# Three products for one: the order of the high and low halves in a chain of retention and two feed-forward layers

## The chip, the cores and the metric

The kernel runs on one core of a Trainium2 chip. The metric is the device time of one execution in microseconds (us); the median of several runs counts. A profile is one further execution, recorded by the hardware profiler.

## The reference

Three stages follow one another. Retention takes q, k and v (4 batches, 8 heads, 576 positions, 64 features per head), weights the scores with powers of a decay per head and multiplies by v. Its output, 2304 tokens by 512 features, goes through a gated layer of 1536 hidden features and a second layer of 2048 hidden features.

```python
# _attn_ref
scores = scale * np.matmul(q, k.transpose(0, 1, 3, 2))
ret = scores * Dmat[None, :, :, :]
return np.matmul(ret, v).astype(np.float32)
# _moe_ref
xn = x / rms * rms_g
g = xn @ w_gate
silu = g * (1.0 / (1.0 + np.exp(-g)))
val = xn @ w_val
return (silu * val @ w_out).astype(np.float32)
# _moe2_ref
h = x @ w_in
g = np.where(pos, h, np.where(neg, 0.0, (h + beta) ** 2 / (4.0 * beta)))
return (g @ w_out).astype(np.float32)
```

## The kernel before

Most products use a number form that is read at one column per cycle but has few bits (`F32R`). To keep the precision, each operand is split into a high half, which is the operand rounded to that form, and a low half, the rest. The helper `split` (lines 294 to 296) has ScalarE write the high half and VectorE subtract it from the source for the low one, so a low half is always finished behind its high half. A product of two operands is then three products into one accumulator: high by high, and twice high by low. The helper `three` (lines 544 to 547) issues them. Its arguments are the stationary operand's halves `wh` and `wl` and the moving operand's halves `xh` and `xl`. It is called in four places:

- `front` (line 557): the gate and the value product of the first layer. Weights stand, the activations `x_t` move (tile `xall`), four triples for the gate and four for the value in each step.
- `back_a` (line 569): the first layer's second product. Weights stand, the hidden activations move (tile `h`). The products are those of the step before.
- `product` (lines 674 to 677): the second layer's first product, seven block products of a Strassen-like scheme, two triples each. Weights stand (`wf`, in the tile `wt`), sums of the activations move (`xall`).
- `back_b` (line 688): the second layer's second product. Here the activations stand (`hh` and `hl`, tile `h`) and the weights move (`wprep`).

The first layer runs over five blocks of 512, 512, 384, 512 and 384 tokens, and in each over 12 steps of 128 hidden features: 24 products in `front`, 12 in `back_a`. Within these steps the pieces of retention for later blocks are put in, and weights for the second layer are prepared. The second layer runs over three batches of 768 tokens with 8 steps each (`step_b`, lines 714 to 764): 42 products of 384 columns in `product`, 36 of 512 in `back_b`. At a change of block `split_x` writes the next block's halves; at a change of batch `split_xb` does.

No order of an engine's queue is written out directly. All calls go to a `Plan`, which knows an estimated cost of each operation and its dependencies. `issue` (lines 139 to 200) plays them through and lets each engine take an operation that is ready: TensorE the first in program order, the others the one with the earliest due time. A due time is computed backwards from the operations that need the result, with TensorE's in their program order (lines 152 to 160). Products into one accumulator stay in order. An operation is taken as ready if it is so within 100 ns (`HOLD`). The order found is then issued to the chip, where each engine works its queue in order and waits on semaphores.

Pairs of products with one stationary operand exist before too: `rms_rstd` (lines 509 and 510) multiplies the high and the low half of the sums of squares by `ones_r`, one behind the other.

```python
nc.tensor.matmul(ps[:, :T], lhsT=ones_r, rhs=hi, start=True, stop=False)
nc.tensor.matmul(ps[:, :T], lhsT=ones_r, rhs=lo, start=False, stop=True)
```

Of the kernel before, what the change touches and what calls it, by code (L numbers as in the profile page):

```python
# [211 lines left out]
def moe_chain_kernel(ctx: ExitStack, tc: tile.TileContext, att, tail, wa, wb, dmat, gq, gk, out):  # L212
    nc = Plan(tc.nc)
# [329 lines left out]

    def three(ps, wh, wl, xh, xl, first, last, **k):
        nc.tensor.matmul(ps, lhsT=wh, rhs=xh, start=first, stop=False, **k)
        nc.tensor.matmul(ps, lhsT=wl, rhs=xh, start=False, stop=False, **k)
        nc.tensor.matmul(ps, lhsT=wh, rhs=xl, start=False, stop=last, **k)

    def front(s, j):
        t = steps[s][1]  # L550
        T = BLOCKS[t]
        fh, fl = a_weights(s, j)
        hi, lo = x_t[t]
        ps = fr_p.tile([P, 512], F32, tag="fr", name="fr")
        for k in range(KD):
            q = slice(k * P, (k + 1) * P)
            three(ps[:, :T], fh[:, q], fl[:, q], hi[:, k, :T], lo[:, k, :T], k == 0, k == KD - 1)
        return ps

    def back_a(s, i):  # L560
        _, t, f = steps[s]
        T = BLOCKS[t]
        oh, ol = a_weights(s, 2)
        hh, hl = h_t[s]
        if f == 0 and i == 0:
            acc_t[t] = [ps_p.tile([P, 512], F32, tag=f"acc{i}") for i in range(KD)]
        ps = acc_t[t][i]
        q = slice(i * P, (i + 1) * P)
        three(ps[:, :T], oh[:, q], ol[:, q], hh[:, :T], hl[:, :T], f == 0, f == NA - 1)
        if f == NA - 1:  # L570
            o = next(o_next)
            nc.scalar.copy(out=o[:, :T], in_=ps[:, :T])
            nc.scalar.dma_start(out=x2d[:, i, STARTS[t]:STARTS[t] + T], in_=o[:, :T])
# [97 lines left out]
    def product(q, j, ps, first, last):  # L671
        w = wf_t[q].rearrange("p (j w k n) -> p j w k n", w=2, k=2, n=P)
        for k in range(2):
            three(
                ps, w[:, j, 0, k], w[:, j, 1, k], xs[:, j, 0, k], xs[:, j, 1, k], first and k == 0, last and k == 1,
                skip_group_check=True,
            )
# [213 lines left out]
```

## Time and profile before

| | |
|---|---|
| time, median of 3 runs | 920.0 us (919.15 to 921.18) |
| the profiled execution's span | 920.9 us |
| products (MATMUL) and their loads (LDWEIGHTS) | 5098 and 5098 |
| TensorE products in flight | 904.3 us, 98% |
| TensorE loads | 797.7 us, 87% |
| VectorE | 576.2 us, 63% |
| ScalarE | 482.3 us, 52% |
| GpSimd | 70.3 us, 8% |

In the profile PE is TensorE with its products, PEld its loads of the stationary operand, which lie beside products, DVE is VectorE, ACT ScalarE, POOL GpSimd, SP the queue that issues most transfers. Products overlap in the records, so the time that one takes in a stream is read from the distance of starts and not from its duration. In the names, `fr<-xall,wt` is a first product of either layer, `acc<-h,wt` a second product of the first layer, `acc<-wprep,h` and `at<-wprep,h` a second product of the second layer, `at<-h,ones_r` the pair with the ones. All operations have one line (L135), that of the planner's call; so one goes by tiles.

### The profile page before, as it was taken

How to read it: one execution, taken by the hardware profiler on the slowest of the kernel's cores; microseconds unless marked ns; L12 is line 12 of the kernel's file. 1: busy time of each engine (PE TensorE's matmuls, PEld its weight loads, DVE VectorE, ACT ScalarE, POOL GpSimd, SP SyncE). 2: the span in 40 equal slices, each digit the busy share in tenths (PEclk: the TensorE clock that was granted, in tenths of full speed). 3: DMA queues.
4: the chain of work that ended last, by engine and by line, in shares of the span. 5: the costliest groups of instructions: out<-in, count | busy, mean ns of one | idle time of the engine just before them, and what ended most of it. 6: DMA issues, size and time to landing. Idle time of an engine off the chain costs nothing.

```text
span 920.9 us, 13342 instructions
## 1 busy us (share of the span) xinstructions
PE 904.3 (98%) x5098; PEld 797.7 (87%) x5098; DVE 576.2 (63%) x929; ACT 482.3 (52%) x858; POOL 70.3 (8%) x80
## 2 busy tenths in 40 slices
PE   8799999999999999999999999999999999999998
PEld 7578888888889998888899998989888998989896
DVE  3978888888988888855658645434734345434343
ACT  3446665555765576533545454445654455644443
POOL 4620001310014001100000000000000000000000
PEclk9999999999999999999999999999999999999999
DMA  9679976988769984642254386646765454755432
GB/s 364 229 261 314 308 278 235 331 331 325 283 240 378 387 291 150 234 150 94 103 202 153 104 329 243 216 160 216 251 222 194 169 191 170 266 165 213 159 137 69
DMA packets 51647, 209.94 MB, mean 228 GB/s; under 512 B 5632, under 2 KB 11392, under 8 KB 47488
## 3 DMA queue, kind: packets, MB, share of 16 engines
q1 hardware_dynamic: 45392, 199.51, 61.2%
q10 hardware_dynamic: 6192, 9.59, 2.8%
q8 instruction: 40, 0.66, 0.3%
q14 instruction: 23, 0.19, 0.1%
HBM read 167.14 MB, written 41.94 MB: 227 GB/s over the span
## 4 chain that ended last, share of the span: by engine, by line
PE 92%; DVE 4%; DMA 2%; ACT 2%; issue 1%; ACTq 0%
PE fr L135 50%; PE acc L135 31%; PE at L135 11%; DMA out_dram<-o 1%; DMA att<-in_att_dram 1%; DVE xraw L135 1%; DVE xall L135 0%; DVE t L135 0%; DMA gk_sb<-in_gk_dram 0%; DVE w L135 0%; DVE wt L135 0%; ACT att L135 0%; DVE state L135 0%; DVE wsum L135 0%; DVE wpair L135 0%
## 5 line engine op out<-in xcount | busy, mean ns | idle before, releaser
L135 PE MATMUL fr<-xall,wt 128*128 128x384 f32 (+1 forms) x2424 | 512.1, 356 | 3.6 <-DVE xall L135 1.3
L135 PEld LDWEIGHTS fr<-xall,wt 128*128 128x128 f32 x2424 | 436.8, 188 | 53.5 <-DVE xall L135 2.4
L135 PE MATMUL acc<-h,wt 128*128 128x512 f32 (+1 forms) x708 | 158.1, 370 | 0.1
L135 PE MATMUL acc<-wprep,h 128*128 128x512 f32 x576 | 155.7, 394 | 0.5 <-ACT h L135 0.5
L135 PEld LDWEIGHTS acc<-h,wt 128*128 128x128 f32 x708 | 128.4, 188 | 18.2 <-ACT o L135 0.6
L135 DVE TENSOR_TENSOR wt<-w,wt 128x512 fp32r<-128x512 f32 (+1 forms) x118 | 114.4, 985 | 17.7 <-ACT wt L135 17.3
L135 PEld LDWEIGHTS acc<-wprep,h 128*128 128x128 f32 x576 | 106.6, 188 | 15.8 <-ACT h L135 0.9
L135 ACT CAST wt<-w 128x512 fp32r<-128x512 f32 (+1 forms) x118 | 96.7, 835 | 42.1 <-PE acc L135 23.6
L135 DVE TENSOR_TENSOR t<-fr,t 128x512 f32<-128x512 f32 (+1 forms) x120 | 76.3, 636 | 58.0 <-PE fr L135 29.5
L135 ACT ACTIVATE att<-att 128x384 f32<-128x384 f32 x156 | 79.2, 523 | 30.1 <-DVE att L135 18.2
L135 ACT CAST h<-t 128x512 fp32r<-128x512 f32 (+1 forms) x60 | 34.6, 577 | 79.3 <-DVE t L135 79.3
L135 DVE TENSOR_TENSOR att<-fr,att 128x384 f32<-128x384 f32 x48 | 26.6, 555 | 70.6 <-ACT att L135 69.6
L135 PE MATMUL at<-wprep,h 128*128 128x512 f32 x288 | 70.3, 392 | 0.0
L135 DVE TENSOR_TENSOR h<-att,h 128x384 fp32r<-128x384 f32 x96 | 52.8, 554 | 23.7 <-ACT h L135 23.1
L135 ACT ACTIVATE t<-fr 128x512 f32<-128x512 f32 (+1 forms) x60 | 33.3, 554 | 59.0 <-PE fr L135 58.7
L135 PEld LDWEIGHTS at<-wprep,h 128*128 128x128 f32 x288 | 53.7, 188 | 10.4
L135 ACT COPY att<-fr 128x384 f32<-128x384 f32 x48 | 23.0, 479 | 75.7 <-PE fr L135 70.2
L135 ACT CAST h<-att 128x384 fp32r<-128x384 f32 x96 | 48.7, 512 | 21.2 <-DVE att L135 20.0
L135 DVE SCALAR_TENSOR_TENSOR att<-att,att 128x384 f32<-128x384 f32 x48 | 26.8, 558 | 42.3 <-ACT att L135 42.3
L135 DVE TENSOR_TENSOR h<-t,h 128x512 fp32r<-128x512 f32 (+1 forms) x60 | 38.0, 634 | 14.2 <-ACT h L135 13.9
L135 DVE SCALAR_TENSOR_TENSOR att<-att,fr 128x384 f32<-128x384 f32 x24 | 13.3, 553 | 36.8 <-ACT att L135 36.8
L135 DVE TENSOR_TENSOR xall<-xraw,xall 128x512 fp32r<-128x512 f32 (+2 forms) x32 | 25.9, 828 | 2.8 <-ACT xall L135 2.4
(144 smaller groups left out, 672.5 us busy)
## 6 DMA issues: line engine op xcount, KB each, us to landing
w<-wa SPq DMA_DIRECT2D x48, 768.0 KB, 4.5
wprep<-wod SPq DMA_DIRECT2D x48, 512.0 KB, 4.0
wt<-wfd SPq DMA_DIRECT2D x24, 1024.0 KB, 5.2
wt<-wfd SPq DMA_DIRECT2D x24, 768.0 KB, 4.5
stage<-in_wb_dram SPq DMA_DIRECT2D x32, 512.0 KB, 6.4
wfd<-wprep SPq DMA_DIRECT2D x8, 1792.0 KB, 7.0
att<-in_att_dram SPq DMA_DIRECT2D x26, 512.0 KB, 5.8
stage<-in_wa_dram SPq DMA_DIRECT2D x26, 512.0 KB, 5.5
```

The lines of the kernel that those rows point to most:

```text
L135: call = lambda: getattr(real, method)(*args, **kwargs)
```

## The change

In `three` the second and the third product change places. Before, the stationary operand's low half by the moving operand's high half came second; now the stationary operand's high half by the moving operand's low half does. The flag that closes the accumulation moves along. Nothing else is edited; the planner computes its order anew.

```diff
     def three(ps, wh, wl, xh, xl, first, last, **k):
         nc.tensor.matmul(ps, lhsT=wh, rhs=xh, start=first, stop=False, **k)
-        nc.tensor.matmul(ps, lhsT=wl, rhs=xh, start=False, stop=False, **k)
-        nc.tensor.matmul(ps, lhsT=wh, rhs=xl, start=False, stop=last, **k)
+        nc.tensor.matmul(ps, lhsT=wh, rhs=xl, start=False, stop=False, **k)
+        nc.tensor.matmul(ps, lhsT=wl, rhs=xh, start=False, stop=last, **k)
```

## Rows read from the trace of the kernel before

**Rows 1.** The page: busy us by engine, and the granted clock in 40 slices.

```profile
PE 904.3 (98%) x5098; PEld 797.7 (87%) x5098; DVE 576.2 (63%) x929; ACT 482.3 (52%) x858; POOL 70.3 (8%) x80
PEclk9999999999999999999999999999999999999999
```

**Rows 2.** Timeline of TensorE, steady first-layer steps: start, length, operation, count.

```profile
100.52 5.60 PE L135 MATMUL fr<-xall,wt 128*128 128x512 f32 x24
108.68 5.60 PE L135 MATMUL fr<-xall,wt 128*128 128x512 f32 x24
...
313.41 4.32 PE L135 MATMUL acc<-h,wt 128*128 128x384 f32 x24
317.57 2.75 PE L135 MATMUL fr<-xall,wt 128*128 128x384 f32 x13
```

**Rows 3.** TensorE's waits, longest first; last row: the only one from 80 to 545.

```profile
PE at L135 <- DMA att<-in_att_dram: 2.2, 1, 2.2
...
PE fr L135 <- DVE wt L135: 0.5, 1, 0.5
```

**Rows 4.** Timeline of TensorE, one step of the second layer, cut to its ends.

```profile
718.13 2.27 PE L135 MATMUL fr<-xall,wt 128*128 128x384 f32 x12
...
733.79 1.40 PE L135 MATMUL fr<-xall,wt 128*128 128x384 f32 x7
```

**Rows 5.** Timelines of TensorE's loads and products, first and last of four ones pairs.

```profile
131.57 0.41 PEld L135 LDWEIGHTS at<-h,ones_r 128*128 128x128 f32 x2
132.03 0.19 PEld L135 LDWEIGHTS acc<-h,wt 128*128 128x128 f32 x1
...
131.80 0.61 PE L135 MATMUL at<-h,ones_r 128*128 128x512 f32 x2
132.25 1.52 PE L135 MATMUL acc<-h,wt 128*128 128x512 f32 x6
...
442.17 0.51 PE L135 MATMUL at<-h,ones_r 128*128 128x384 f32 x2
442.52 1.32 PE L135 MATMUL acc<-h,wt 128*128 128x512 f32 x5
```

**Rows 6.** Timeline of the opening; the last row is of the chain that ended last.

```profile
37.73 0.96 PE L135 MATMUL fr<-xall,wt 128*128 128x512 f32 x3 [0.28 <-ACT xall L135]
...
42.05 0.50 PE L135 MATMUL fr<-xall,wt 128*128 128x512 f32 x1 [1.35 <-DVE xall L135]
...
54.29 3.01 PE fr L135 x12
```

**Rows 7.** Timeline of the block changes at 149 and 354 us.

```profile
147.19 1.89 DVE L135 TENSOR_TENSOR xall<-xraw,xall 128x512 fp32r<-128x512 f32 x3
149.93 2.88 PE L135 MATMUL fr<-xall,wt 128*128 128x512 f32 x12
...
353.76 2.11 DVE L135 TENSOR_TENSOR xall<-xraw,xall 128x512 fp32r<-128x512 f32 x3
354.35 0.94 PE L135 MATMUL fr<-xall,wt 128*128 128x512 f32 x3
```

**Rows 8.** Timeline of a wait for low weights in the first layer.

```profile
304.22 0.62 PE L135 MATMUL fr<-xall,wt 128*128 128x384 f32 x2
305.33 8.24 PE L135 MATMUL fr<-xall,wt 128*128 128x384 f32 x46 [0.49 <-DVE wt L135]
```

**Rows 9.** Timeline of the last second products.

```profile
910.42 0.98 ACT L135 CAST h<-att 128x384 fp32r<-128x384 f32 x2 [0.21 <-DVE att L135]
910.98 3.73 PE L135 MATMUL acc<-wprep,h 128*128 128x512 f32 x15 [0.45 <-ACT h L135]
```

**Rows 10.** Timeline of TensorE's restarts at the first batch change.

```profile
671.89 1.32 PE L135 MATMUL fr<-xall,wt 128*128 128x384 f32 x6 [0.54 <-DVE att L135]
675.09 0.79 PE L135 MATMUL fr<-xall,wt 128*128 128x384 f32 x3 [0.49 <-ACT d_sb L135]
676.11 1.15 PE L135 MATMUL fr<-xall,wt 128*128 128x384 f32 x5 [0.23 <-DVE att L135]
```

## The prediction

> **What bounds the kernel now.** I read the busy table first, then the granted clock, then the waits of TensorE, then the starts of its products. TensorE has products in flight for 904.3 of 920.9 us; VectorE, the next, for 576.2; the clock stands at its upper level (2.4 GHz, tenths of 9) in all 40 slices [rows 1]. A busy TensorE need not be a full one, so the starts decide. Where only 512 columns are in play, one step of the first layer is 24 products and then 12, and starts repeat every 8.16 us (100.52 to 108.68): 226.7 ns each. With 384 columns 24 products take 4.16 us (313.41 to 317.57): 173.3 each [rows 2]. The 128 columns between cost 53.3 ns, one column per cycle at 2.4 GHz, and both leave 13.3 ns per product that isn't streaming. So TensorE is bound by its columns plus a fixed 13.3 ns. Its listed waits are 2.2 us or less each; from 80 to 545 us only one of 0.5 us is listed [rows 3]. One step of the second layer takes 15.66 us (718.13 to 733.79) for 42 products of 384 and 36 of 512, which at the two prices is 42 x 173.3 + 36 x 226.7 = 15.44 us: 0.22 us over, no listed wait in it [rows 4].
>
> **The change, part by part.** It adds and removes no product. The first layer has 60 steps x 12 triples, the second 24 x 26: 720 + 624 = 1344 triples, each with a second product that newly has the stationary operand of the first.
>
> *What sharing is worth.* Columns stay, so only the fixed 13.3 ns could go: at most 1344 x 13.3 = 17.9 us. That it goes needs either a load that is dropped or a load that is cheaper the second time. The trace has this very case four times, from 131.8 to 442.2 us: the sums of squares are multiplied by one matrix of ones, high half and then low half, back to back in the same number form. Both products have a load record of their own (x2 at 131.57) [rows 5]. From the first product of a pair to the product behind the pair, the first of the four takes 0.45 us (131.80 to 132.25, 512 columns) and the last 0.35 (442.17 to 442.52, 384 columns); at the usual prices these would be 2 x 226.7 = 453 and 2 x 173.3 = 347 ns [rows 5]. Sharing saved nothing there. And the loads are hidden already: the load for the product at 132.25 runs from 132.03 for 0.19 us, wholly inside the product before it [rows 5]. Value 0; the ends are 0 and -17.9 us, and I take the first since these rows are the operation itself. (One thing they lack: the second load of each pair waits on VectorE's low half, so they can't exclude that loads without a wait of their own are merged.)
>
> The Trainium skill (TensorE: Matmul & The Clock Gate, "What overlaps and what doesn't") says that a load overlaps products in flight only when the row group differs. Here all products use all 128 rows, so by it each load of 0.19 us [rows 5] would stand between two products, and 1344 dropped loads would give, as an estimate by that page, 1344 x 0.19 = 255 us. This trace disagrees: the load at 132.03 lies inside a product of the same rows [rows 5], and 190 ns of load behind 213 ns of columns don't fit into 226.7. A chance of its own would be under 0.01; it is held in that of the first rival.
>
> *The low activations are wanted one product earlier* in the first products of both layers and in the first layer's second products (there the activations move and the weights stand). Behind a product that waits, the weight-low product and all of TensorE's later ones are queued, and the sigmoid on ScalarE waits for the triple's end. Price where the low half is what TensorE waits for: one product, 227 or 173 ns. In the opening this is so: the first three products go at 37.73 on high halves, and before 42.05 TensorE waits 1.35 us for VectorE's `xall`, a low half [rows 6]. A weight-low product that ran ahead of that wait now runs behind it: +0.23 us. But the chain that ends last goes over VectorE there (its xraw and xall pieces) and comes back to TensorE only at 54.29 [rows 6]; with that cover it is 0, and if each of four chunks paid, 4 x 0.227 = +0.9. I take +0.2, one product, because only one wait of that length is shown. At the block change at 149 us the last low halves end at 147.19 + 1.89 = 149.08 and the first product that wants them starts at 149.93: 0.85 us of cover against 0.23 taken. At the one near 354 us halves land until 353.76 + 2.11 = 355.87 while the products already run in small groups (x3 at 354.35) between those of retention, with no listed wait [rows 3, 7]: cover is other work; 0, or +0.23 without it.
>
> *The low weights are wanted one product later.* At 304.22 two products go and then TensorE waits for VectorE's `wt`, the low weights, until 305.33 [rows 8]. One more product of 173 ns fits ahead of that wait: -0.17, at worst 0. In the second layer's second products the computed activations stand, so there it is their low half that comes later. At the end ScalarE casts high halves from 910.42 on and TensorE restarts behind the first, at 910.98; the 15 products then run without a listed wait for a low half [rows 9], so the gain is 0, at best one product, -0.23. I take 0.
>
> *Buffers.* The last reader of a high half of the activations is now the third product of its triple instead of the second, so the ScalarE cast that overwrites it can start 173 ns later, at the two batch changes of the second layer, seven casts each. The overwritten half is next read about one 15.66 us step later [rows 4]: 0.
>
> *The planner's order.* The order of each queue is computed from due times, and a due time moves by a product. Ties on VectorE and ScalarE can fall the other way, in places I can't see in the trace of before. The nearest rows are the waits at the first batch change, 671.89, 675.09 and 676.11, which end on VectorE or ScalarE freeing an accumulator: 0.54 + 0.49 + 0.23 = 1.26 us listed [rows 10]. They could go or come double: -1.3 to +1.3; no row favours either sign, so 0. The second layer's excess of 0.22 us per step has no releaser; 24 x 0.22 = 5.3 us, and an order of operands could move a part of it either way. First-layer steps in steady flow show no such excess (both widths leave the same 13.3 ns [rows 2]) although they have the same triples, so the triple isn't its likely cause: 0, with a quarter of it, 1.3 us, either way for the range.
>
> Sum: +0.2 - 0.17 = about 0: 920.9 us of span again. The three runs have a median of 920.0, 0.9 below this profiled execution, and I forecast 920.0.
>
> **The rivals.**
> *A load is dropped or cheaper.* For it: the loads of new pairs mostly need no wait of their own, unlike the four pairs. Against it: the pairs' 0.45 and 0.35 us [rows 5]. 920.0 - 17.9 = 902.1 us. Chance 0.04.
> *Slower: the low half of the activations ends the wait.* It decides where a low half lands later than the product ahead of it ends. The places are the opening (0.9), the block changes (4 x 0.23 = 0.9) and the two batch changes (2 x 7 x 0.173 = 2.4): 4.2 us if all pay, 2.1 if half do, so 922.1 to 924.2. For it: the opening waits on such a half today. Against it: 0.85 us of cover at 149 us, and the other block change fills with attention. Chance 0.11.
> *Faster by the planner's order.* The 1.26 us of the batch change, the wait of 0.5 at 305.33 and 0.3 of the opening go: 920.0 - 2.1 = 917.9 us. Chance 0.08.
> *The change does nothing that can be measured.* My forecast, 0.77.
>
> **How the numbers follow.** A measurement of this kernel tells about 0.2% from no change, 1.84 us. Faster 0.04 + 0.08 = 0.12; same 0.77; slower 0.11. Bounds of the unknown costs around 920.0, not all at one end: 1.3 of order and 1.3 of the second layer's excess make 1.8 when independent, and the opening adds 0.7 above. The range from 917.9 to 922.2 takes in the planner's gain and the lower half of the slower rival; the dropped load stays out.
>
> **What would show it.** As many loads as products, and 8.16 us per first-layer step: sharing is worth nothing. Fewer load records or steps under 8.16: the first rival. A longer wait of TensorE on xall in the opening, or new ones behind block and batch changes: the second. Waits gone at 304, 671 to 676 us: the third. A second-layer step off 15.66 us by more than 0.06 would show that operand order moves its excess (24 x 0.06 = 1.4 us), which I put at 0. I am wrong above all if loads with no wait of their own behave otherwise than the four pairs.

## The result and the profile after

The changed kernel takes 925.53 us in the median of 4 runs (923.65 to 926.67), beside 919.99 in 4 runs of the kernel before: 1.0054 times as long, 95% interval 1.0038 to 1.0069. Measured again in 12 runs it took 924.41 against 921.02, a ratio of 1.0032 (1.0017 to 1.0047). It is slower by 3.4 to 5.5 us. The forecast was no change, 920.0 with a range up to 922.2, so it was wrong.

First the sums of the page: busy us by engine, and the granted clock in 40 slices. The profiled execution took 923.65 us with a span of 921.9.

```profile
PE 906.7 (98%) x5098; PEld 798.3 (87%) x5098; DVE 574.9 (62%) x929; ACT 481.2 (52%) x858; POOL 69.1 (7%) x80
PEclk9999999999999999999999999999999999999999
```

There are still as many loads as products, 5098 of each, with as much time in loads as in [rows 1], so no load was dropped. The steady steps say the same. This is the timeline of TensorE, a first-layer step and then the ends of a second-layer step (start, length, operation, count):

```profile
107.50 5.60 PE L135 MATMUL fr<-xall,wt 128*128 128x512 f32 x24
...
115.66 2.66 PE L135 MATMUL fr<-xall,wt 128*128 128x512 f32 x11
...
719.07 2.27 PE L135 MATMUL fr<-xall,wt 128*128 128x384 f32 x12
...
734.75 1.57 PE L135 MATMUL fr<-xall,wt 128*128 128x384 f32 x8
```

A first-layer step takes 115.66 - 107.50 = 8.16 us, as in [rows 2]. A second-layer step takes 15.68, where [rows 4] gave 15.66. What the change was most likely to move stands still.

The waits of TensorE do move (engine, tile and what it waited for: us in total, times, longest):

```profile
PE fr L135 <- DVE xall L135: 2.1, 2, 1.4
PE fr L135 <- DVE wt L135: 1.6, 3, 0.7
PE at L135 <- DMA att<-in_att_dram: 1.6, 1, 1.6
...
PE fr L135 <- DVE t L135: 0.3, 1, 0.3
```

In [rows 3] there was one wait of 0.5 us for VectorE's `wt`, the low halves of the weights. Now there are three, 1.6 us together, and one for `t`. All four lie between 301 and 334 us, in the third block (384 tokens). The list leaves out a wait under 0.15 us and counts a product as running until its modelled end. TensorE's loads show more (waits of the loads from 285 to 340 us, before and then after):

```profile
PEld fr L135 <- DVE wt L135: 1.2, 2, 0.8
```

```profile
PEld fr L135 <- DVE wt L135: 3.0, 4, 1.0
...
PEld fr L135 <- DVE t L135: 0.6, 1, 0.6
```

The products in the trace of after:

```profile
299.90 0.85 PE L135 MATMUL fr<-xall,wt 128*128 128x384 f32 x4
300.59 0.86 PE L135 MATMUL acc<-h,wt 128*128 128x384 f32 x4
302.14 3.75 PE L135 MATMUL fr<-xall,wt 128*128 128x384 f32 x20 [0.69 <-DVE wt L135]
...
316.61 0.86 PE L135 MATMUL fr<-xall,wt 128*128 128x384 f32 x4
318.11 4.17 PE L135 MATMUL fr<-xall,wt 128*128 128x384 f32 x22 [0.64 <-DVE wt L135]
322.53 0.62 PE L135 MATMUL fr<-xall,wt 128*128 128x384 f32 x2 [0.25 <-DVE t L135]
...
333.25 3.76 PE L135 MATMUL fr<-xall,wt 128*128 128x384 f32 x20 [0.32 <-DVE wt L135]
336.85 0.39 PE L135 MATMUL at<-h,ones_r 128*128 128x512 f32 x1
```

Four products of a step now go ahead of the low weights (high by high and high by low, for gate and value), then TensorE stops. In [rows 8] only two went ahead. So the new triple does what it says, it asks for the low weights later, but VectorE brings them later still, counted from the start of the step that needs them. Its timeline, before and then after:

```profile
315.70 1.23 DVE L135 TENSOR_TENSOR wprep<-wpair,wprep 128x1024 fp32r<-128x1024 f32 x1 [0.39 <-ACT wprep L135]
316.84 1.82 DVE L135 TENSOR_TENSOR wt<-w,wt 128x1024 fp32r<-128x1024 f32 x2
...
318.92 1.82 DVE L135 TENSOR_TENSOR wt<-w,wt 128x1024 fp32r<-128x1024 f32 x2
```

```profile
314.96 0.43 DVE L135 TENSOR_SCALAR wpair<-wpair 128x512 uint32<-128x512 uint32 x1 [0.73 <-ACT wpair L135]
315.42 1.50 DVE L135 SCALAR_TENSOR_TENSOR wpair<-stage,wpair 128x512 uint32<-128x512 uint32 x1
316.84 1.81 DVE L135 TENSOR_TENSOR wt<-w,wt 128x1024 fp32r<-128x1024 f32 x2
...
322.39 1.22 DVE L135 TENSOR_TENSOR wt<-w,wt 128x1024 fp32r<-128x1024 f32 x1
...
323.99 0.68 DVE L135 TENSOR_TENSOR wt<-w,wt 128x512 fp32r<-128x512 f32 x1
```

A pair of `wt` is the low halves of one step. Before, VectorE served the pairs of two steps by 320.7. After, the first pair starts at the same 316.84, behind second-layer preparation (`wpair`), although its step starts at 316.61 instead of 317.57; the second pair waits until 322.39, behind more of that preparation and `t`. The end of the first half of each pair, counted from the start of its step's first product (us; ahead of it with a minus):

| first-layer step | before | after |
|---|---|---|
| 29 | 1.05 | 2.18 |
| 31 | 0.49 | 1.44 |
| 32 | -1.93 | 1.89 |
| 33 | 0.75 | 1.81 |

In this stretch VectorE has little room. Busy time from 299 to 334 us, before and then after (length, then PE, PEld, DVE, ACT, POOL busy with counts, clock, DMA share, GB/s):

```profile
299.00:334.00 35.00, 34.48 (x211) 33.40 (x209) 30.82 (x50) 21.29 (x33) 1.30 (x2) 1.00 0.90 339
```

```profile
299.00:334.00 35.00, 32.88 (x188) 29.73 (x187) 28.69 (x47) 18.62 (x30) 1.04 (x1) 1.00 0.89 340
```

VectorE is busy 30.82 of 35 us before, 88%. The share alone does not mark the stretch: in the same trace it is 88% from 60 to 149 us too (78.05 of 89) and 86% from 149 to 281 (113.16 of 132), where nothing is lost. What marks it is the margin of the low weights: in the steps 14 to 27 of before their first half ends 1.85 to 8.47 us ahead of its step, in the steps 28, 29, 31 and 33 it ends 0.49 to 1.05 behind the first product. TensorE's idle time grows from 0.52 to 2.12, and it has 188 products in the stretch instead of 211.

How much of the loss is here? A clean measure is the time from the first product of the 27th first-layer step to that of the 41st (from 281 to 395 us): in all kernels of this study the same products start in between. It is 113.37 us before and 117.10 after, 3.73 more. A second trace of each gives 113.71 and 117.01. So 3.3 to 3.7 us of the measured 3.4 to 5.5 arise here.

The listed waits are only a part of that. Counted from start to start against the steady 173.3 and 226.7 ns, the products ahead of the four waits and those right behind them lose 3.1 us after, and those at the one wait of before 0.76: 2.35 of the 3.73. Another 0.9 lies at changes between groups of products, most of it at waits too short for the list: TensorE waits for `wt` a fourth time, 0.148 us, before 323.66. And 0.7 lies in retention's products, which are issued in smaller groups here.

The 20 steps ahead of it take 180.68 in both first traces and the 18 behind it 128.78, the same to the last digit. The opening adds a little: from the first product of the first layer to its second step it is 17.08 us after and 16.56 before, in the second traces 16.97 and 16.57, so 0.4 to 0.5 more.

The rest of a trace moves by its own: when the opening's products can start differs between two traces of one kernel by over a microsecond, with its input transfers. That is why the profiled spans differ by only 1.0: the trace of before has a wait of 2.2 us for an input in the opening [rows 3], that of after 1.6, and the waits at the batch change [rows 10] are gone. In a further trace of the kernel before they are gone as well (18 products in one go from 670.38), so their absence is not the change's doing.

### The profile page after: what moved, and what is told of

Same layout as the page of the kernel before. It is cut to its first block, busy times and chain, and to the rows that moved or that the text cites. A ratio compares the mean times of both kernels' runs of the same rounds, so it can differ in the third digit from the quotient of the medians.

```text
span 921.9 us, 13375 instructions
## 1 busy us (share of the span) xinstructions
PE 906.7 (98%) x5098; PEld 798.3 (87%) x5098; DVE 574.9 (62%) x929; ACT 481.2 (52%) x858; POOL 69.1 (7%) x80
## 4 chain that ended last, share of the span: by engine, by line
PE 92%; DVE 3%; DMA 2%; issue 1%; ACT 1%; POOL 0%; ACTq 0%; DVEq 0%
PE fr L135 50%; PE acc L135 30%; PE at L135 11%; DMA wa<-w 1%; DMA att<-in_att_dram 1%; DVE wt L135 1%; DVE xraw L135 1%; DMA gk_sb<-in_gk_dram 0%; DVE xall L135 0%; DVE w L135 0%; DVE wprep L135 0%; DVE t L135 0%; DVE ret L135 0%; ACT sq L135 0%; ACT wpair L135 0%
## 5 line engine op out<-in xcount | busy, mean ns | idle before, releaser
L135 DVE TENSOR_TENSOR wt<-w,wt 128x1024 fp32r<-128x1024 f32 (+1 forms) x118 | 111.6, 960 | 22.1 <-ACT wt L135 21.8
L135 ACT CAST wt<-w 128x1024 fp32r<-128x1024 f32 (+1 forms) x118 | 96.4, 834 | 46.6 <-PE acc L135 31.6
L135 ACT ACTIVATE att<-fr 128x384 f32<-128x384 f32 x24 | 11.8, 490 | 27.9 <-PE fr L135 27.7
```

The costliest lines, as they stand in the source:

```text
L135: call = lambda: getattr(real, method)(*args, **kwargs)
```

## The experiments

Two theories stood against each other. *The queues:* the planner drew a new order of all queues, and VectorE's part in it makes TensorE wait; another draw may do better or worse with either triple. *The triple:* the new order of products costs by itself, whatever the draw, and then every planner setting should show the same 3 to 4 us. The first was held after the comparison of the two traces.

Set side by side, the orders differ far more than "ties" would. Compared by operation and tile, buffer numbers left out, the traces of before and after have 330 lines of difference in the 929 operations of VectorE, 250 in ScalarE's 858 and 260 in TensorE's 5098 products. Two traces of one kernel have none.

### Triple and queues exchanged

The planner was given two books of the same operations, book 0 with the old triple and book 1 with the new one. `PLAN` names the book whose plan orders every queue, `DO` the book that is issued. The issuing loop only keeps dependencies in order.

```diff
+PLAN, DO = {'all': 0}, 1
...
+        plans = [self.order(book) for book in (0, 1)]
...
+        queues = {e: [i for i in plans[PLAN.get(e, PLAN["all"])] if self.books[0][0][i][0] == e] for e in engines}
```

The new triple with the queues planned for the old one:

> The products are those of the change (stationary high half twice in a row), but every engine's queue stands in the order that the planner found for the triples of before, position by position. Theory Q (the 5.5 us are the recomputed order of the queues): 920 us, within 1.5. Theory T (the order inside the triple costs on TensorE itself, by its operands or by the earlier wait for the low activations): 925.5 us, with a wait of TensorE for xall that is longer than before in the opening and at block changes. Both halves: in between.

Measured: 925.89 us (8 runs), ratio 1.0052 (1.0034 to 1.0070). The old triple with the queues planned for the new one, `PLAN, DO = {'all': 1}, 0`:

> The reverse: the products inside each triple stand as before, and every queue in the order that the planner found for the changed triples. Theory Q: 925.5 us, within 1.5, and TensorE waits for the low halves of the weights (wt from VectorE) at 300 to 335 us as after the change. Theory T: 920 us. If the low weights wait is a matter of both, it is longer here than after the change, by one product of 173 ns at each wait, since the low weights are wanted one product earlier: 926 to 927.

Measured: 939.31 us (4 runs), ratio 1.0194 (1.0170 to 1.0218). By the number alone the first fits the triple's theory (925.5) and not the queues' (920), and no theory gave 939.3: so what the queues' theory expected was missed twice. But neither kernel is before or after with one cause taken out, as this pair was meant to be. Each mismatch makes waits of its own. With the old queues and the new triple, TensorE stops at low halves that the new triple asks for one product earlier (timeline of TensorE):

```profile
327.82 0.34 PE L141 MATMUL acc<-h,wt 128*128 128x384 f32 x1
328.74 0.97 PE L141 MATMUL acc<-h,wt 128*128 128x384 f32 x4 [0.58 <-DVE h L141]
...
349.07 0.80 PE L141 MATMUL acc<-h,wt 128*128 128x384 f32 x3 [0.85 <-DVE h L141]
```

That is the prediction's rival of the low half, in `back_a` and not at the block changes where it was looked for. It explains only a part: steps 27 to 40 take 114.87 us here, 1.2 to 1.5 more than in the two traces of before. The largest part in this trace is at the first batch change, where the restarts of [rows 10] wait 0.94, 1.48 and 0.22 us and the granted clock is then 0.50 from 680 to 683; those waits differ between two traces of the kernel before too, so how much of them is the exchange's doing stays open. With the new queues and the old triple, the low weights are late in seven places (waits of TensorE; then its timeline):

```profile
PE fr L141 <- DVE wt L141: 7.5, 7, 1.9
```

```profile
303.68 0.34 PE L141 MATMUL fr<-xall,wt 128*128 128x384 f32 x1
305.89 1.09 PE L141 MATMUL fr<-xall,wt 128*128 128x384 f32 x3 [1.87 <-DVE wt L141]
```

Steps 27 to 40 take 122.73 us there, and behind the wait of 1.87 us the granted clock is 0.57 from 306 to 310. So the queues are laid out to the product for their own triple: a half wanted one product, 0.17 us, before its due time costs a wait.

### The two kernels again

The same kernels written through the two books, the changed one in 12 runs and the one before in one.

> The changed kernel once more, for a second trace, since its profiled execution was the fastest of four and lies only 1.0 us of span above that of before. All theories: 925.5 us within 1.5. Theory Q: TensorE's waits for wt from VectorE at 300 to 335 us stand again (1.6 us listed in the first trace), and the rest of the loss is waits that differ from one execution to the next.

> The kernel before once more, for a second trace: the profiled execution of before (span 920.9 us) lies about 1.7 us above what its median of 921.0 us leaves for a span, by the 1.8 us that lie between span and time in every run of the last job. Expected: a span of 918 to 920 us, with an opening that is about 1 us shorter, as in the four other traces, or without the three waits at the first batch change.

Measured: 924.41 us (12 runs), ratio 1.0032 (1.0017 to 1.0047), and 922.03 in the one run of the kernel before, beside a median of 921.06. The changed kernel's second trace has the same 1.6 us of waits for `wt` in three places, so they belong to its order and not to one execution.

### Due times exchanged

The new triple in the plan and on the chip, but the due times that rank VectorE's, ScalarE's and the other queues' work computed from the old triple's book:

```diff
+    def order(self, book):
+        ops = self.books[0][0]
...
             due[i] = late - ops[i][3]
+        ops = self.books[book][0]
```

> The changed triples, but the due times by which VectorE and ScalarE choose are computed from the triples of before; the play-through (who is ready when) is that of the changed ones. Theory D (the shifted due times of the low halves make VectorE late with the low weights at 300 to 335 us): 920 to 921.5 us, and the waits for wt there are under 0.7 us as before. Theory W (the order of before is a favourable draw, and any redrawn order costs, wherever it comes from): 922 to 932 us, with waits in other places.

Measured: 922.95 us (11 runs), ratio 1.0021 (1.0007 to 1.0034). That is above the 920 to 921.5 expected if the due times were all, though the waits at issue are gone. The trace lists no wait of TensorE from 285 to 340 us, and VectorE again serves two pairs of `wt` close together (TensorE, then VectorE):

```profile
304.58 7.90 PE L141 MATMUL fr<-xall,wt 128*128 128x384 f32 x44
...
316.48 8.73 PE L141 MATMUL fr<-xall,wt 128*128 128x384 f32 x48
```

```profile
316.00 1.83 DVE L141 TENSOR_TENSOR wt<-w,wt 128x1024 fp32r<-128x1024 f32 x2 [0.17 <-ACT wt L141]
...
318.08 1.82 DVE L141 TENSOR_TENSOR wt<-w,wt 128x1024 fp32r<-128x1024 f32 x2
```

So the new triple can run without these waits. Next, the due times of only one step's operations (the fifth step, some 85 to 92 us) were taken from the other book, in both directions:

```diff
+FROM, TO = 4, 5
...
+        mixed = [due[DO][:a] + due[1 - DO][a:b] + due[DO][b:]] * 2
```

New triple, with that one step's old due times:

> The changed kernel, but with the due times of the triples of before for the operations of one single step, the fifth of the first layer (about 85 to 92 us). No wait of TensorE stands in that stretch. The play-through after it falls otherwise: about a third of VectorE's rows, and TensorE's order of steps 24 to 34 becomes nearly that of the run with all due times of before. Cascade theory (a small shift in the opening redraws everything behind it, and the 3.4 us lost at 300 to 333 us are a consequence of the draw): the waits for wt there are gone as in that run, and the time is 921.5 to 924, below the 924.4 of the changed kernel. Local theory (the due times of the low weights cost where they are used): the waits at 301, 317 and 333 us stand, 924.4 within 1.

Measured: 923.51 us (12 runs), ratio 1.0024 (1.0013 to 1.0036); no wait listed from 285 to 340 us. Old triple, with that one step's new due times:

> The reverse: the triples of before with the changed due times for the operations of that one step alone. Cascade theory: a redraw, 922 to 935 us, with waits in stretches far behind 92 us. Local theory: 921 within 1, as before.

Measured: 925.01 us (12 runs), ratio 1.0036 (1.0025 to 1.0048). The old triple now loses as much as the new one, and waits for `wt` in the same places (steps 27 to 40 take 116.19 us):

```profile
302.53 4.11 PE L143 MATMUL fr<-xall,wt 128*128 128x384 f32 x22 [0.75 <-DVE wt L143]
...
317.27 0.62 PE L143 MATMUL fr<-xall,wt 128*128 128x384 f32 x2
318.43 4.26 PE L143 MATMUL fr<-xall,wt 128*128 128x384 f32 x23 [0.54 <-DVE wt L143]
```

These two runs settle the waits at 301 to 334 us: they appear with the old triple and vanish with the new one, and a change of due times at 85 to 92 us decides, 200 us ahead. A few choices taken otherwise early change the order far behind them.

They do not settle the whole loss. Both new-triple kernels without the waits still take 1.9 and 2.4 us more than before. Steps 27 to 40 take 114.73 and 114.81 us there, 1.0 to 1.4 above the two traces of before, although no wait is listed. The timeline of TensorE shows most of the reason, before and then with the old due times (the run with one step's old due times has the same):

```profile
361.48 1.16 PE L135 MATMUL at<-att 64*128 64x128 f32 x16
362.57 2.38 PE L135 MATMUL acc<-h,wt 128*128 128x384 f32 x12
```

```profile
358.14 1.16 PE L141 MATMUL at<-att 64*128 64x128 f32 x8
359.23 3.02 PE L141 MATMUL fr<-xall,wt 128*128 128x512 f32 x12
362.18 1.16 PE L141 MATMUL at<-att 64*128 64x128 f32 x8
363.26 2.38 PE L141 MATMUL acc<-h,wt 128*128 128x384 f32 x12
```

Sixteen of the 64-row products of retention take 1.09 us in a row, and eight of them take 1.09 us too. The sixteen start two by two, some 6 ns apart, the eight one by one, some 110 ns apart. The planner, which prices each of them alone (`cost`), has parted the partners here. That costs 1.08 us and is no wait of any kind. Retention's other products, in smaller groups here too, bring it to 1.6 to 1.8 us, while the 0.76 us of the wait in the trace of before is saved.

### Other draws: the planner's constants

A small change of a planner constant leaves the triple alone and draws the order anew. Four settings were tried with both triples: `PE_LATENCY` 190 and 170, `HOLD` 90 and 110. The edits are of this form:

```diff
-    LATENCY, PE_LATENCY = 120, 180
+    LATENCY, PE_LATENCY = 120, 190
```

```diff
-    HOLD, COLD = 100, 6800
+    HOLD, COLD = 90, 6800
```

> The kernel before with one constant of the planner nudged, the latency it assumes behind TensorE, from 180 to 190 ns; the triples are untouched. It reorders the queues in some places (VectorE's in about a sixth of its rows). Theory Q in its wide form (the order of before is a lucky one, and any reordering costs): 921 to 926. Theory Q in its narrow form (what costs is the due time of the low halves): 920 within 1.5. Theory T: 920.

> The changed triples with the planner's constant that the run before last nudged (190 instead of 180 ns behind TensorE), so that both kernels of a pair are redrawn: the old triples took 932.3 us there. Theory W: 922 to 935 us, above or below 932.3, the sign being chance. Theory T2 (matched to its own queues, the changed triple costs some 4 us whatever the order): 936 us.

> The triples of before with another constant of the planner nudged: an operation counts as ready if it is so within 90 ns instead of 100. It reorders about an eighth of VectorE's rows. Theory W: 922 to 935 us. Theory D: 920 to 921.5, since the triples and so the due times of the halves are those of before; the 932.3 us of the last nudge would then belong to that constant alone.

> The changed triples with the 90 ns instead of 100 that the run with the triples of before took 925.9 us with. Theory W (any order is a draw): 922 to 935, either side of 925.9. Theory T2 (the changed triple costs about 4 us in any order): 930.

> Old triple, HOLD 110 instead of 100: partner of the run with the new triple and HOLD 110, which took 926.3. Theory (a redraw of the queues, of either sign): 921 to 932, and the difference of the two triples may have either sign. Rival (the new triple costs 3 to 4 us of its own in any draw): 922 to 924.

> The changed triples with 110 ns instead of 100: one more draw for the changed triple. Theory W: 921 to 933 us, and the waits of TensorE stand in other places than at 301, 317 and 333 us or have other lengths.

> Old triple, the planner's PE_LATENCY 170 instead of 180. Theory (a redraw): 921 to 932, above the kernel before with 9 chances in 10 since that one is the best of all draws so far. Rival (only large changes of the constants redraw the order): 920 to 922.

> New triple, PE_LATENCY 170: partner of the run of the old triple with 170. Theory (a redraw of either sign): the difference to the partner is anything from -6 to +6 us. Rival (the triple costs 3 to 4 us of its own): 3 to 4 us above the partner.

Measured (medians in us of 6 runs, 12 for hold 110 with the old triple, both of latency 170 and the new triple as given, 19 for the old one as given; in brackets the ratio to the kernel before, measured along with it):

| planner | old triple | new triple | new less old |
|---|---|---|---|
| as given | 921.02 | 924.41 (1.0032) | +3.4 |
| latency 170 | 920.60 (0.9994) | 924.45 (1.0042) | +3.9 |
| hold 110 | 920.91 (1.0006) | 926.33 (1.0049) | +5.4 |
| hold 90 | 925.87 (1.0054) | 930.16 (1.0094) | +4.3 |
| latency 190 | 932.34 (1.0115) | 927.15 (1.0080) | -5.2 |

Which of these are new draws is seen by setting the traces' orders beside each other, as above. Latency 170 changes no line of TensorE's and VectorE's orders with the old triple, and 12 lines of TensorE's and 2 of VectorE's with the new one: it repeats the pair as given, and the difference with it. Hold 110 leaves the old order nearly whole (34 lines on VectorE) and the time with it. So nearly the same order gives the same time, within 0.5 us, three times over. The other settings are draws (200 lines on VectorE with hold 90 and 252 with latency 190, old triple), and the old triple's time goes up by 4.8 and 11.3 us in them. Two of the numbers are those of the other theory: hold 90 with the new triple came at the 930 us that a cost of the triple's own gave, and latency 170 at 3.9 above its partner, where 3 to 4 was that theory's; latency 190 came at 927.15 where it gave 936. The expectation that the old triple would be slower with latency 170, since the kernel before was the best draw so far, missed, because that was no draw.

A large part of these losses lies in another place. With latency 190 (old triple) TensorE waits in the opening, where before it waited 1.28 us for the same tile:

```profile
50.00 0.43 PE L135 MATMUL at<-t,att 128*64 128x128 f32 x2 [2.01 <-DVE t L135]
...
55.72 1.22 PE L135 MATMUL fr<-xall,wt 128*128 128x512 f32 x2 [1.38 <-DVE t L135]
...
58.88 3.77 PE L135 MATMUL fr<-xall,wt 128*128 128x512 f32 x10
```

Behind the first of the two waits the granted clock falls (stretches as above):

```profile
50.00:51.00 1.00, 1.00 (x7) 0.58 (x9) 0.99 (x3) 0.98 (x1) 0.00 (x0) 1.00 1.00 397
52.00:61.00 9.00, 7.62 (x25) 5.80 (x24) 4.36 (x9) 3.78 (x7) 2.19 (x3) 0.50 0.47 163
62.00:66.00 4.00, 4.00 (x48) 3.52 (x47) 2.69 (x4) 3.31 (x7) 1.58 (x2) 1.00 0.63 242
```

From 52 to 61 us it is 0.50 of full speed, the lower level of 1.2 GHz, and the ten products from 58.88 to 62.49 take 361 ns each instead of 226.7. In the trace of before the clock is 1.00 in all these stretches. At the third step this kernel is 5.2 us behind before's trace; the same wait, of 1.8 us, and the same fall are there with hold 90 (6.6 behind). Steps 27 to 40 add 3.8 with latency 190 (117.13) and 0.2 with hold 90 (113.59). The new triple has the fall with hold 90 too (0.50 from 58 to 62 us) and not with latency 190 (1.00 from 50 to 80), in the executions that were traced. The mean granted clock of the other runs with latency 190 is low with either triple (0.990 to 0.994 with the old, 0.990 to 0.996 with the new), so how much of the -5.2 is this fall stays open.

### Low weights given an earlier due time

In the changed kernel, each VectorE operation that writes `wt` was made due 1.5 us earlier:

```diff
+        if engine == "vector" and out.tensor.name.startswith("wt"):
+            self.early.add(i)
...
-            due[i] = late - ops[i][3]
+            due[i] = late - ops[i][3] - (1500 if i in self.early else 0)
```

> New triple; in the planner each VectorE operation that writes a low half of the weights (tile wt) is given a due time 1.5 us earlier, nothing else. Theory (the loss between 299 and 333 us is VectorE serving the weights' low halves behind other work, in an order that the due times draw): the listed waits of TensorE for wt in that stretch, 1.6 us in three places after the change, are gone or under 0.4, and the part of the loss that hangs on them, 3.4 us, comes back; but the order is redrawn everywhere, so the time is 918 to 928 and not sure to fall. Rival (the new triple itself makes TensorE wait for low halves, whatever VectorE's order): waits for wt of 1 us or more stay in the stretch.

Measured: 925.13 us (12 runs), ratio 1.0046 (1.0026 to 1.0066). The waits for `wt` sink from 1.6 to 0.7 us, less than expected, and waits for `h` come in their place:

```profile
320.33 0.96 PE L137 MATMUL acc<-h,wt 128*128 128x384 f32 x4 [0.59 <-ACT h L137]
322.23 1.66 PE L137 MATMUL acc<-h,wt 128*128 128x384 f32 x8 [0.94 <-DVE h L137]
...
325.24 8.01 PE L137 MATMUL fr<-xall,wt 128*128 128x384 f32 x44 [0.66 <-DVE wt L137]
```

Steps 27 to 40 take 116.81 us, against 117.10. Where VectorE has only an eighth of its time free, putting one operation first puts another late: it is the whole order that has to fit.

### What stays open

Whether the new triple makes a bad order more likely, or costs something in any order, is not settled. Of four unlike orders for the old triple two keep steps 27 to 40 within 113.4 to 113.7 us (as given, hold 90) and two do not (116.19 and 117.13). All seven for the new triple lie above, at 114.73 to 119.33. One thing the seven share: retention's products, from start to start, take 0.6 to 2.2 us more in these steps than in the trace of before, against 0 to 0.85 in the four orders of the old triple. The longest, 119.33 (hold 110), also has two waits of 1.44 and 1.65 us and a granted clock of 0.50 from 322 to 324 us behind them. Three unlike pairs with equal settings have the sign of the result and one has the other, which leaves room for both. Nor was any order found that beats the kernel before.

## Why the prediction was wrong, point by point

**What bounds the kernel.** Right. TensorE stays at 98%, and both kinds of steady step keep their length.

**What sharing is worth: 0.** Right. There are 5098 loads for 5098 products, and 8.16 us per step. The doubt it kept, that loads with no wait of their own might be merged, is answered by the 1344 new pairs: no. On this the trace of after disagrees again with the Trainium skill (TensorE: Matmul & The Clock Gate, "What overlaps and what doesn't"), by which loads of the same row group lie between products: 798.3 us of loads and 906.7 us of products fit into a span of 921.9.

**Low activations one product earlier: +0.2.** Of the right sign and too small. In the opening `xall` is waited for twice, 2.1 us together, where one wait of 1.3 stood, and the way to the second step is 0.4 to 0.5 us longer. The new wait takes 0.72 us, and behind the two the granted clock is 0.50 from 41 to 43 us in both traces of after and 1.00 in both of before; part of this is covered, since the 1.28 us that before waits for `t` at 48.40 are gone. The two block changes show no new wait. The mechanism itself is real, as the exchange with the old queues showed (1.4 us for `h`), but the planner draws the queues for the triple that it gets.

**Low weights one product later: -0.17.** This step failed. It took VectorE's order around 304 us as given and let TensorE gain a product on it. Of the gain, the four products ahead of the wait instead of two are there to be seen. But VectorE's order was not the same any more, one wait became three with a fourth for `t`, and steps 27 to 40 lost 3.3 to 3.7 us, 2.35 of them at these waits.

**The planner's order: 0, between -1.3 and +1.3.** This is the step that decided, and its size was wrong: steps 27 to 40 alone measured +3.3 to +3.7. It was priced by the nearest waits that end on VectorE, those of the batch change [rows 10], as if a few ties could fall otherwise around them. The order was redrawn from the opening on, and the loss came in the stretch where VectorE has little room, not at the batch change. A sign was at hand: the wait for `wt` [rows 8], which says that VectorE's order is just in time there, with VectorE busy for 30.82 of 35 us. The busy share by itself would not have told. Draws with the triple left alone gave +3.9, +4.8 and +11.3 us. Nor is there a reason for 0 as the middle: of the unlike orders tried for the old triple the one before is the best by 4 us, so another one was likely to be worse; that is an argument from four orders, and no bound. The third rival saw the planner's order as a gain only.

**The second layer's excess: 0.** Nearly right: 15.68 beside 15.66 us. The last batch shows the same 0.03 per step: from its first step to its last it is 110.18 us in both traces of after and 109.98 and 109.97 in those of before. If all 24 steps do so, that is some 0.7 us, as an estimate.

**The rivals.** The dropped load did not come. Slower by the low half named the right sign and about the right time (up to 924.2), by luck: its half is the wrong one. It was the weights' low halves in the steps, not the activations' at the changes; only its opening showed, with 0.4 to 0.5 us.

## What to carry to other kernels

Where a planner computes the queues, an edit in the program's order redraws all of them, and that can cost more than the edit is worth. Look for the stretch in which a second engine has little time free and its results arrive just in time, take the spread of the time over a few planner constants as the measure of such an edit, and expect a loss rather than zero when the present order is one of the better ones. To tell a cause from a draw, exchange the due times and leave the program alone: to exchange the queues themselves makes waits of its own.

## What the runs showed of the hardware

- The first product behind a wait of TensorE brings 0.11 us more than the wait: in the trace of after, the 20 products from 302.14 and from 333.25 take 3.59 and 3.60 us to the next start, where 20 times 173.3 ns are 3.47. Its own load starts together with it there (302.138 and 302.140), while in steady flow a load lies inside the product before it; that this is what adds is likely and was not tried.
- Products of 64 rows that stand next to a partner start some 6 ns behind it and cost nothing more: 16 take 1.09 us, 8 without partners the same 1.09.
- A wait of TensorE can cost its clock besides. With latency 190 and the old triple a wait of 2.01 us in the opening was followed by a granted clock of 0.50 from 52 to 61 us; this and the waits put that kernel 5.2 us behind by the third step. A wait of 1.87 us was followed by 0.57 from 306 to 310 (new queues, old triple), waits of 1.44 and 1.65 by 0.50 from 322 to 324 (hold 110, new triple). The waits of 0.69, 0.64 and 0.32 us in the trace of after left it at 1.00 from 299 to 334.
